# Attention with a top-1 expert layer on one core: where the softmax denominators' key sums are added, and when ScalarE takes the router's products out of PSUM

## The chip, the cores and the metric

The kernel runs on one core of a Trainium2 chip. The metric is device microseconds for one execution. Three runs of the kernel before took 587.34, 593.33 and 595.07 us; the median is 593.33 us.

## The reference

There are two stages. The first is attention with a tanh cap on the scores, over 4 batches, 12 heads, 448 positions and a head size of 64. Its output is laid out as 1792 tokens of 768 numbers. The second is a mixture of 8 experts (768 to 1024 to 768, relu) of which each token takes the best one, by the cosine between the token and an expert's embedding.

```python
def _attn_ref(q, k, v, cap) -> np.ndarray:
    scale = 1.0 / np.sqrt(q.shape[-1])
    scores = scale * np.matmul(q, k.transpose(0, 1, 3, 2))
    scores = cap * np.tanh(scores / cap)
    scores = scores - np.max(scores, axis=-1, keepdims=True)
    attn = np.exp(scores)
    attn = attn / (np.sum(attn, axis=-1, keepdims=True) + 1e-09)
    return np.matmul(attn, v).astype(np.float32)
...
    logits = xn @ en.T / tau
    expert_idx = np.argmax(logits, axis=1)
...
        h = np.maximum(x[mask] @ w1[e], 0.0)
        out[mask] = gate_w[mask, None] * (h @ w2[e])
```

All is in float32. With the cap, the maximum need not be subtracted, so the kernel takes the exponentials as they are and divides at the end.

## The kernel before, in words

**Attention.** The 48 heads are 24 pairs of heads, and two pairs make a group: 12 groups (`NH`). A group is worked off in seven blocks (`STEPS`), u = 0 to 6. Blocks 0 to 2 are the first pair's keys 0 to 383, 128 keys at a time for both heads; blocks 3 to 5 are the same for the second pair; block 6 holds the last 64 keys of both pairs. A block of `prob` is 128 keys x 2 heads x 448 queries. Keys lie on partitions, so the softmax denominator is a sum over blocks and then over partitions.

One loop over a slot number g puts the instructions of all engines in order (`manual_schedule`: what stands first in the program stands first in its engine's queue). In slot g the program issues:

- `scores(g)`: TensorE multiplies K by Q (six matmuls, from parts that VectorE splits into high and low in `split_qk`), and ScalarE takes the tanh and then the exponential. From block pair 4 on the exponential is one instruction for two blocks;
- `values(g - 4)`: TensorE adds the block's product with V in PSUM. After a group's block 6, in slot u = 3 of the next group, VectorE copies the two results out (`xt`, line 850). The two PSUM banks of results are single buffers, so the next group's first `values`, in slot u = 4, waits for that copy;
- `add_keys(g - 3)`: the key sums, below;
- up to two steps of a queue `later`: the router, its transposes, and `rows`, which transposes `xt` and scales it;
- from about group 8 on, one step of `fill`: half of a 128-row piece of the first expert's weights is split into two float16 parts, by ScalarE (line 227) and VectorE (line 228).

**Key sums.** For each pair of heads, `add_keys` makes one tile `sums` of 128 x 896. Blocks 0 and 1 are added on VectorE (line 807). Block 2 is added by a DMA that accumulates into `sums`, issued from GpSimd's queue (line 812), and so is the half of block 6 that belongs to the pair (line 821, 64 partitions). Only in the last group are blocks 5 and 6 added by VectorE and GpSimd (lines 815 and 823). A second accumulation into a tile waits for the first to land, and GpSimd's queue waits with it. A buffer of `prob` holds two blocks and there are four, so the tanh eight slots later waits until the accumulations from that buffer have landed.

**Router.** `router` (line 856) multiplies the attention output by the expert embeddings and the key sums by a column that picks them: 12 matmuls for two groups at once, or 6 for one group, eight times in all. It stands in slot u = 4 of the group after the one that it needs, behind that slot's scores and values on TensorE. ScalarE copies the product from PSUM to `ls` in the same step (line 870). `router_t`, one slot later, transposes `ls` on TensorE (lines 881, 882), and VectorE takes the reciprocal of the sums (line 886) and scales the logits. The steps after it are `rows`.

**Experts.** After attention the tokens are sorted by expert, and tiles of 128 tokens go through the two layers as float16 products in three parts. `tile0` begins the first tile at the end of attention.

Of the kernel before, what the change touches and what calls it, by code (L numbers as in the profile page):

```python
# [35 lines left out]
ALU = mybir.AluOpType  # L36
# [48 lines left out]
def attention_moe(ctx: ExitStack, tc: tile.TileContext, q, k, v, cap, emb, tau, w1, w2, qk_pairs, v_pairs, out):  # L85
    nc = tc.nc
# [189 lines left out]
    with ExitStack() as actx:  # L276
# [77 lines left out]
        NH = B * NP // 2  # L354
# [393 lines left out]
        def attention_bounded(apool, ps_s, ps_o):  # L748
# [20 lines left out]
            def block(g):  # L769
                return prob[g // 2][:, 2 * (g % 2) : 2 * (g % 2) + 2, :]  # L770
# [32 lines left out]
            def add_keys(g):  # L803
                i, u = divmod(g, STEPS)
                if u in (1, 4):
                    t = apool.tile([P, 2, S], F32, tag="sums", name=f"sums{2 * i + u // 3}", bufs=6)
                    nc.vector.tensor_tensor(t, block(g - 1), block(g), op=ALU.add)  # L807
                    sums[2 * i + u // 3] = t
                elif u in (2, 5):
                    t = sums[2 * i + u // 3]  # L810
                    if i < NH - 1 or u == 2:
                        nc.gpsimd.dma_start(out=t, in_=block(g), accum_op=ALU.add)  # L812
                    else:
                        for s, eng in enumerate((nc.vector, nc.gpsimd)):
                            eng.tensor_tensor(t[:, s, :], t[:, s, :], block(g)[:, s, :], op=ALU.add)
                elif u == STEPS - 1:
                    for n in range(2):
                        sl = slice(n * DH, (n + 1) * DH)
                        t = sums[2 * i + n]
                        if i < NH - 1:  # L820
                            nc.gpsimd.dma_start(out=t[sl], in_=block(g)[sl], accum_op=ALU.add)  # L821
                        else:
                            (nc.gpsimd if n else nc.vector).tensor_tensor(t[sl], t[sl], block(g)[sl], op=ALU.add)

            def values(g):
                i, u = divmod(g, STEPS)
# [29 lines left out]
            def router(i, n):  # L856

                d = ps_t.tile([P, 512], F32, tag="t", name=f"lp{i}")
                far = n if n == 2 else 0
                for a in range(3):  # L860
                    for m in range(n):
                        k = m + far if a else m
                        nc.tensor.matmul(  # L863
                            d[k * 32 : (k + 1) * 32, :S],
                            pick[:, a - 1, :] if a else en_t[:, (i + m) % NP, :, :].rearrange("p a e -> p (a e)"),
                            sums[i + m][:, a - 1, :] if a else xt[i + m],
                            start=a == (1 if a and far else 0), stop=a == (0 if far and not a else 2),
                        )
                ls = apool.tile([P, S], F32, tag="lrow", name=f"ls{i}", bufs=1)
                nc.scalar.copy(ls, d[:, :S])  # L870
                return ls
# [43 lines left out]
            route = []  # L915
# [16 lines left out]
            def after(i):  # L932

                tmp = {}
                (b, m), nop = divmod(i, NP // 2), lambda: None
                if m == 0:
                    return
                j, n = (2 * i - 2, 4) if m == 1 else (2 * i, 2)
                steps = [lambda: tmp.update(l=router(j, n)), lambda: router_t(j, n, tmp["l"])]
                steps += [lambda x=x: rows(x) for x in range(j, j + n)]  # L940
                if m == NP // 2 - 1:
                    steps.append(lambda: write_rows(b, 0, D))
                    if b < B - 1:
                        steps += [
                            lambda: (square_x(b, 0), square_x(b, 1), hold.extend([1] * HOLD)),
                            lambda: (square_x(b, 2), square_x(b, 3), norms_x(b), side.extend(z), hold.extend([1] * HOLD)),
                        ]
                        z = [nop, nop, lambda: (scales_x(b), route.extend(g))]
                        r = [lambda: choose(b), nop, nop, nop, lambda: rank_rows(b, rank(b))]
                        if b == B - 3:  # L950
                            r += [
                                lambda: tmp.update(m=first_expert(counts(b))),
                                lambda: (first_order(tmp["m"]), first_scales(), start_first()),
                            ]
                        if b == B - 2:
                            r.append(lambda: tmp.update(b=first_rows(counts(b))))
                        r += [lambda: (add_carry(b), token_rows(b, range(2))), lambda: token_rows(b, range(2, 4))]
                        g = [lambda: gates(b), lambda: gates_out(b)]
                        if b == B - 2:
                            g += [nop, lambda: first_table(tmp["b"])]  # L960
                        steps.insert(2, lambda: route.extend(r))
                later.extend(steps)

            with tc.manual_schedule():
# [717 lines left out]
```

## Time and profile before

| | |
|---|---|
| median of three runs | 593.33 us (587.34 to 595.07) |
| profiled execution | 591.52 us, of which the profile's span is 589.8 us |
| TensorE matmul busy in the span | 481.3 us (82%) |
| VectorE, ScalarE, GpSimd busy | 286.3, 295.6, 171.8 us |
| granted TensorE clock, mean | 0.933 of full speed |

Names in the rows: PE is TensorE's matmul, PEld its weight load, DVE VectorE, ACT ScalarE, POOL GpSimd. A number in square brackets at the end of a timeline row is the idle time of the engine just before, and what ended it. Attention runs from about 8 us to 280 us, the experts after it. In the trace, a group's block 6 is the one whose scores have line 790.

### The profile page before, as it was taken

To read this page: it belongs to the slowest core of one execution; us is meant where nothing else is said; L and a number is where in the kernel's file an instruction comes from. 1 tells how busy PE (TensorE), PEld (TensorE's weight loads), DVE (VectorE), ACT (ScalarE), POOL (GpSimd) and SP (SyncE) were. 2 spreads that over 40 slices of the span, in tenths; PEclk is the share of its full clock that TensorE was granted. 3 is DMA by queue.
4 is the path that set the end of the run, shared out by engine and by line. 5 is a ranking of instruction groups with operands and counts; after the bars stand their busy time and mean duration, and the time that the engine had idled before them with its cause. 6 is when DMAs were issued, how large, how long until landed. Compare 5 with 4: busy or idle time off the path is not lost. (4 is left out here: it accounts for less than half of the span.)

```text
span 589.8 us, 11987 instructions
## 1 busy us (share of the span) xinstructions
PE 481.3 (82%) x4621; PEld 295.7 (50%) x4622; DVE 286.3 (49%) x694; ACT 295.6 (50%) x350; POOL 171.8 (29%) x267
## 2 busy tenths in 40 slices
PE   4988893998849595575777979999999999997970
PEld 2323330343213142122646738887778887786750
DVE  4552564264634466327656591266221851295810
ACT  3975784776937498641530641173111821284500
POOL 3111212111120211414010462265322563255420
PEclk9997998899988899777979989999999999998986
DMA  7586779775993858541506992148111672096920
GB/s 206 145 182 101 158 215 228 115 162 166 171 247 88 202 189 157 125 74 55 175 5 227 396 345 108 56 163 314 55 55 56 229 287 62 31 326 236 364 100 6
DMA packets 34045, 97.06 MB, mean 165 GB/s; under 512 B 7998, under 2 KB 8282, under 8 KB 33955
## 3 DMA queue, kind: packets, MB, share of 16 engines
q1 hardware_dynamic: 24818, 66.14, 32.0%
q0 software_dynamic: 7888, 28.21, 23.7%
q10 hardware_dynamic: 1248, 1.61, 0.9%
q8 instruction: 44, 0.72, 0.5%
q14 instruction: 47, 0.38, 0.2%
HBM read 67.94 MB, written 13.00 MB: 137 GB/s over the span
## 5 line engine op out<-in xcount | busy, mean ns | idle before, releaser
L794 ACT ACTIVATE prob<-s,icap 128x896 f32<-128x896 f32 x84 | 82.5, 995 | 28.2 <-PE s L784 12.7
L237 PEld LDWEIGHTS <-h 128*128 128x128 f16 x1056 | 79.9, 99 | 11.2 <-issue 8.9
L237 PE MATMUL h<-xh,h 128*128 128x128 f16 (+1 forms) x480 | 78.7, 218 | 6.3 <-issue 4.9
L798 ACT ACTIVATE prob<-prob,cap_b 128x896 f32<-128x896 f32 (+1 forms) x57 | 79.8, 1399 | 1.9
L237 PE MATMUL h<-xl,h 128*128 128x128 f16 (+1 forms) x480 | 78.7, 218 | 1.5 <-issue 1.5
L237 PE MATMUL h<-xh,l 128*128 128x128 f16 (+1 forms) x480 | 78.7, 218 | 0.3 <-issue 0.3
L836 PE MATMUL v<-prob,vb 128*64 128x448 f32 x288 | 73.3, 589 | 4.1 <-DVE xt L850 4.1
L784 PE MATMUL s<-hi 64*128 64x448 f32 x144 | 35.4, 489 | 27.9 <-ACT prob L794 19.2
L812 POOL DMA_DIRECT2D sums<-prob x23 | 21.3, 927 | 109.0 <-DVE sums L807 25.9
L237 PEld LDWEIGHTS <-l 128*128 128x128 f16 x528 | 52.0, 99 | 0.5 <-issue 0.5
L784 PEld LDWEIGHTS s<-hi 64*128 64x128 f32 x144 | 14.2, 193 | 69.7 <-ACT prob L794 35.8
L210 POOL TENSOR_TENSOR x_tile<-xg 128x768 f32<-128x768 f32 x16 | 24.3, 1520 | 82.0 <-PE xt L218 67.7
L863 PE MATMUL lp<-sums,pick 128*32 128x448 f32 x96 | 30.0, 726 | 21.8 <-DMA sums<-prob 21.8
L1405 PE MATMUL h<-xh,h 128*128 128x160 f16 x192 | 41.0, 237 | 6.7 <-PEq L1548 4.1
L249 ACT ACTIVATE hh<-h 128x512 f16<-128x512 f32 (+1 forms) x20 | 11.5, 575 | 69.7 <-PE h L237 69.7
L221 ACT CAST xh<-xt 128x384 f16<-128x384 f32 x30 | 13.0, 482 | 64.1 <-PE xt L218 56.2
L250 DVE SCALAR_TENSOR_TENSOR hl<-h,hh 128x512 f16<-128x512 f32 (+1 forms) x20 | 13.3, 664 | 64.3 <-ACT hh L249 64.3
L643 PEld LDWEIGHTS <-hh 128*128 128x128 f16 (+1 forms) x352 | 33.3, 101 | 20.0 <-issue 2.0
L228 DVE SCALAR_TENSOR_TENSOR l<-w1r,by_pos,h 128x1024 f16<-128x1024 f32 x30 | 37.7, 1307 | 11.3 <-ACT h L227 11.3
L821 POOL DMA_DIRECT2D sums<-prob x22 | 21.0, 955 | 73.2 <-DMA sums<-prob 56.8
L1405 PE MATMUL h<-xl,h 128*128 128x160 f16 x192 | 41.1, 237 | 0.0
L1405 PE MATMUL h<-xh,l 128*128 128x160 f16 x192 | 41.1, 238 | 0.0
(309 smaller groups left out, 1037.2 us busy)
## 6 DMA issues: line engine op xcount, KB each, us to landing
w1r<-in_moe_w_dram SPq DMA_DIRECT2D x36, 512.0 KB, 6.2
w2r<-in_moe_w_dram SPq DMA_DIRECT2D x24, 768.0 KB, 7.1
sums<-prob POOLq DMA_DIRECT2D x23, 448.0 KB, 6.7
qkb<-in_qk_pairs_dram SPq DMA_DIRECT2D x11, 896.0 KB, 5.8
vb<-in_v_pairs_dram SPq DMA_DIRECT2D x12, 448.0 KB, 5.5
sums<-prob POOLq DMA_DIRECT2D x22, 224.0 KB, 4.4
x_dram<-xsb SPq DMA_DIRECT2D x4, 1152.0 KB, 5.4
ring<-in_moe_w_dram SPq DMA_DIRECT2D x6, 512.0 KB, 3.8
```

What stands on the lines that cost most here:

```text
L210: nc.gpsimd.tensor_tensor(x_tile, xg[:, :D], xg[:, SCALE : SCALE + 1].to_broadcast([P, D]), op=ALU.mult)
L228: nc.vector.scalar_tensor_tensor(out=lo, in0=raw, scalar=scale, in1=hi, op0=ALU.mult, op1=ALU.subtract, accum_out=acc)
L237: nc.tensor.matmul(hp[:, f, :W], l[j][:, c], x[:, j, :W], start=j == 0 and f == 0 and n == 0, stop=j == DC - 1 and f == 3 and n == 2, skip ...
L643: nc.tensor.matmul(y, hidden[h][l][:, c, o : o + k], w2p[p % 2][w][f // 2][:, f % 2, m * C : (m + 1) * C], start=f == 0 and n == 0, stop=f ...
L784: nc.tensor.matmul(sp[:, s, :S], l[sl, kc], r[sl, :], start=n == 0, stop=n == 2)
L794: nc.scalar.activation(o, sp[:, :, :S], AF.Tanh, scale=icap)
L798: nc.scalar.activation(o, o, AF.Exp, scale=cap_b)
L812: nc.gpsimd.dma_start(out=t, in_=block(g), accum_op=ALU.add)
L821: nc.gpsimd.dma_start(out=t[sl], in_=block(g)[sl], accum_op=ALU.add)
L836: nc.tensor.matmul(o[sl, :S], vb[:, u, sl], pt[:, s, :], start=u % 3 == 0, stop=False, skip_group_check=True)
L863: nc.tensor.matmul(d[k * 32 : (k + 1) * 32, :S], pick[:, a - 1, :] if a else en_t[:, (i + m) % NP, :, :].rearrange("p a e -> p (a e)"), su ...
L1405: nc.tensor.matmul(o, w1p[p % 2][l][j][:, c], x[:, j, :], start=j == 0 and f == fs[0] and m == 0, stop=j == DC - 1 and f == fs[-1] and m == 2,
```

## The change

All the additions of `add_keys` are put on VectorE, as `tensor_tensor` instructions, in the slots where the DMAs were issued; none is left on GpSimd or a DMA. The router's step is cut in two: the matmuls stay in their slot, and ScalarE's copy becomes a step of its own in the next one. All later steps of that queue (transposes, `rows`, the choice of experts) move by one place.

```diff
                 elif u in (2, 5):
                     t = sums[2 * i + u // 3]
-                    if i < NH - 1 or u == 2:
-                        nc.gpsimd.dma_start(out=t, in_=block(g), accum_op=ALU.add)
-                    else:
-                        for s, eng in enumerate((nc.vector, nc.gpsimd)):
-                            eng.tensor_tensor(t[:, s, :], t[:, s, :], block(g)[:, s, :], op=ALU.add)
+                    nc.vector.tensor_tensor(t, t, block(g), op=ALU.add)
                 elif u == STEPS - 1:
                     for n in range(2):
                         sl = slice(n * DH, (n + 1) * DH)
                         t = sums[2 * i + n]
-                        if i < NH - 1:
-                            nc.gpsimd.dma_start(out=t[sl], in_=block(g)[sl], accum_op=ALU.add)
-                        else:
-                            (nc.gpsimd if n else nc.vector).tensor_tensor(t[sl], t[sl], block(g)[sl], op=ALU.add)
+                        nc.vector.tensor_tensor(t[sl], t[sl], block(g)[sl], op=ALU.add)
...
+                return d
+
+            def router_c(i, d):
                 ls = apool.tile([P, S], F32, tag="lrow", name=f"ls{i}", bufs=1)
                 nc.scalar.copy(ls, d[:, :S])
                 return ls
...
-                steps = [lambda: tmp.update(l=router(j, n)), lambda: router_t(j, n, tmp["l"])]
+                steps = [
+                    lambda: tmp.update(d=router(j, n)),
+                    lambda: tmp.update(l=router_c(j, tmp["d"])),
+                    lambda: router_t(j, n, tmp["l"]),
+                ]
...
-                        steps.insert(2, lambda: route.extend(r))
+                        steps.insert(3, lambda: route.extend(r))
```

In the program of the change the lines behind `add_keys` have other numbers: 811 and 816 are the new additions, 843 is the copy `xt`, 866 the router's copy, 901 is in `rows`.

ScalarE, in the group that runs the first router, slots u = 4 to 6; `s_4`, `s_5`, `s_6` are the scores of blocks 4 to 6 of that group, `lp` the router's product. Before:

```order
L794 ACTIVATE prob_529<-s_4_530,icap 128x896
L870 COPY ls_560<-lp_547 128x448
L794 ACTIVATE prob_529<-s_5_562,icap 128x896
L798 ACTIVATE prob_529<-prob_529,cap_b 128x1792
L794 ACTIVATE prob_585<-s_6_586,icap 128x896
```

and in the change:

```order
L794 ACTIVATE prob_529<-s_4_530,icap 128x896
L794 ACTIVATE prob_529<-s_5_560,icap 128x896
L798 ACTIVATE prob_529<-prob_529,cap_b 128x1792
L866 COPY ls_572<-lp_547 128x448
L794 ACTIVATE prob_574<-s_6_575,icap 128x896
```

The copy has moved behind the next slot's tanh and the exponential of the two blocks.

VectorE, in the next group, from the first sum of slot u = 0 to the copies of slot u = 3; `xsb<-xb` is the scaling in `rows`. Before:

```order
L807 TENSOR_TENSOR sums_624<-prob_499,prob_529 128x896
L905 TENSOR_TENSOR xsb<-xb_628,inv_574 128x3x128
L905 TENSOR_TENSOR xsb<-xb_628,inv_574 64x128
L905 TENSOR_TENSOR xsb<-xb_647,inv_574 128x3x128
L905 TENSOR_TENSOR xsb<-xb_647,inv_574 64x128
L850 COPY xt_680<-v_542 128x448
L850 COPY xt_682<-v_621 128x448
```

and in the change:

```order
L807 TENSOR_TENSOR sums_617<-prob_499,prob_529 128x896
L901 TENSOR_TENSOR xsb<-xb_621,inv_583 128x3x128
L901 TENSOR_TENSOR xsb<-xb_621,inv_583 64x128
L811 TENSOR_TENSOR sums_617<-sums_617,prob_529 128x896
L901 TENSOR_TENSOR xsb<-xb_640,inv_583 128x3x128
L901 TENSOR_TENSOR xsb<-xb_640,inv_583 64x128
L816 TENSOR_TENSOR sums_545<-sums_545,prob_574 64x896
L816 TENSOR_TENSOR sums_617<-sums_617,prob_574 64x896
L901 TENSOR_TENSOR xsb<-xb_660,inv_583 128x3x128
L901 TENSOR_TENSOR xsb<-xb_660,inv_583 64x128
L843 COPY xt_680<-v_542 128x448
L843 COPY xt_682<-v_614 128x448
```

Three additions more stand ahead of the copies `xt` (the fourth of a group stands in slot u = 5), and one more step of `rows`, which came in the slots before.

## Rows read from the trace of the kernel before

**Rows 1.** The page, part 1: busy us, share of the span, instructions.

```profile
PE 481.3 (82%) x4621; PEld 295.7 (50%) x4622; DVE 286.3 (49%) x694; ACT 295.6 (50%) x350; POOL 171.8 (29%) x267
```

**Rows 2.** Windows (stretch: length, busy us by engine, clock, DMA share, GB/s).

```profile
32.55:154.23 121.68, 102.02 (x604) 38.45 (x602) 56.65 (x128) 85.74 (x85) 21.96 (x27) 0.93 0.77 170
154.23:260.91 106.68, 75.99 (x428) 26.44 (x428) 49.66 (x147) 68.93 (x79) 22.43 (x28) 0.87 0.67 155
...
310.00:589.80 279.80, 245.61 (x3148) 199.28 (x3148) 130.08 (x273) 98.21 (x127) 110.13 (x162) 0.96 0.49 180
```

**Rows 3.** Waits, whole span: who waited for whom, us in total, times, longest.

```profile
ACT ls L870 <- PE lp L863: 54.1, 8, 12.7
...
DVE inv L886 <- PE lt L882: 56.8, 7, 15.3
...
PE lp L863 <- DMA sums<-prob: 21.8, 11, 6.3
...
PE s L784 <- ACT prob L794: 19.2, 13, 6.7
...
ACT prob L794 <- DMA sums<-prob: 12.5, 3, 8.0
```

**Rows 4.** Timeline of the longest router: start, us, instruction, [idle before, releaser].

```profile
172.29 0.59 DVE L763 CAST hi<-qkb 128x832 fp32r<-128x832 f32 x1 [6.43 <-DMA qkb<-in_qk_pairs_dram]
...
177.35 3.11 PE L863 MATMUL lp<-sums,pick 128*32 128x448 f32 x10 [1.10 <-DMA sums<-prob]
...
180.39 0.47 PE L784 MATMUL s<-hi 64*128 64x448 f32 x2
```

**Rows 5.** Windows of seven routers, first product to next scores; columns as above.

```profile
112.64:116.32 3.68, 3.29 (x27) 0.80 (x25) 2.07 (x3) 2.01 (x2) 0.98 (x2) 1.00 0.32 31
...
244.89:258.48 13.59, 7.93 (x26) 1.30 (x24) 0.78 (x1) 0.95 (x1) 2.97 (x5) 0.63 0.79 138
sum 55.38, PE 33.62 PEld 6.44 DVE 12.93 ACT 10.92 POOL 10.24; mean PE 4.80 PEld 0.92 DVE 1.85 ACT 1.56 POOL 1.46
```

**Rows 6.** Timeline of the shortest router.

```profile
114.72 1.66 PE L863 MATMUL lp<-sums,pick 128*32 128x448 f32 x10 [0.39 <-DMA sums<-prob]
```

**Rows 7.** Timeline: scores behind a tanh that waited for an accumulation.

```profile
45.53 0.74 PE L784 MATMUL s<-hi 64*128 64x448 f32 x2 [3.74 <-ACT prob L794]
...
103.53 0.74 PE L784 MATMUL s<-hi 64*128 64x448 f32 x2 [6.67 <-ACT prob L794]
```

**Rows 8.** Groups of instructions, VectorE: xcount, busy us, mean ns, idle before.

```profile
L764 DVE TENSOR_TENSOR lo<-qkb,hi 128x832 fp32r<-128x832 f32 x24 | 24.6, 1026 | 0.8
...
L228 DVE SCALAR_TENSOR_TENSOR l<-ring,first_s,h 128x384 f16<-128x384 f32 (+1 forms) x28 | 21.8, 786 | 20.6 <-ACT h L227 20.6
...
L905 DVE TENSOR_TENSOR xsb<-xb,inv 128x384 f32<-128x384 f32 (+1 forms) x48 | 17.4, 412 | 6.1 <-PE xb L901 6.1
...
L763 DVE CAST hi<-qkb 128x832 fp32r<-128x832 f32 x24 | 14.0, 582 | 8.5 <-DMA qkb<-in_qk_pairs_dram 8.5
...
L807 DVE TENSOR_TENSOR sums<-prob 128x896 f32<-128x896 f32 x12 | 13.0, 1084 | 0.0
...
L870 ACT COPY ls<-lp 128x448 f32<-128x448 f32 x8 | 4.3, 534 | 54.1 <-PE lp L863 54.1
...
L823 DVE TENSOR_TENSOR sums<-sums,prob 64x896 f32<-64x896 f32 x1 | 1.1, 1076 | 0.0
```

**Rows 9.** Window of one group with VectorE densely filled.

```profile
209.30:226.28 16.98, 13.83 (x96) 5.68 (x95) 14.94 (x49) 16.72 (x24) 1.71 (x2) 1.00 0.75 227
```

**Rows 10.** Timeline of the last group's additions.

```profile
268.39 2.09 POOL L823 TENSOR_TENSOR sums<-sums,prob 64x896 f32<-64x896 f32 x1 [0.72 <-DVE sums L815]
...
268.75 2.14 DVE L228 SCALAR_TENSOR_TENSOR l<-ring,first_s,h 128x384 f16<-128x384 f32 x1
...
275.77 0.96 PE L863 MATMUL lp<-xt,en_t 128*32 128x448 f32 x2 [6.29 <-DVE xl L222]
```

**Rows 11.** DMA issues: KB each, median us to landing.

```profile
sums<-prob POOLq DMA_DIRECT2D x23, 448.0 KB, 6.7
```

## The prediction

> **What bounds the kernel now.** I read the busy times first, to see which engine could be the bound. TensorE is busy for 82% of the span, VectorE for 49%, ScalarE for 50%, GpSimd for 29% [rows 1]. A mean over stages says little, so next come the windows [rows 2]. From 310 us on, in the experts, TensorE is busy for 245.6 of 279.8 us, and no line of the change runs there; I take that stage as shifted, not changed. The attention groups lie in two windows: 32.55 to 154.23 us, without the splitting of the first expert's weights (`fill`), and 154.23 to 260.91 us, with it. In the first TensorE is busy for 102.0 of 121.7 us, in the second only for 76.0 of 106.7 us, and there the granted clock has fallen to 0.87. No engine fills the second window: it is a stage of waits.
>
> The table of waits names them [rows 3]. TensorE stood for 21.8 us in the router's matmuls, waiting for a DMA that accumulates the key sums, and for 19.2 us in scores, waiting for ScalarE's tanh to free a PSUM buffer; ScalarE's tanh itself waited 12.5 us for such a DMA, because the block of `prob` was still being read. The two longest rows, ScalarE's copy waiting for the router (54.1 us) and VectorE waiting for the transposes (56.8 us), are consequences: both engines stand because TensorE is held in the router. The timeline of the longest router shows the chain and its second price: the last matmuls ran only at 177.35, took 3.11 us for ten that need 1.66 us in another router, and the next scores began at 180.39 [rows 4, 6]. The half-speed stretch, after a wait, has a granted clock of 0.63 over another such router [rows 5].
>
> **The change part by part, against the profiled execution of 591.52 us.**
>
> *Routers.* From a router's first matmul to the next scores, seven of the eight took 55.38 us together [rows 5]. The shortest, with 12 matmuls, took 3.68 us of which 0.39 us was a wait [rows 5, 6], so 3.29 us is the price without one; I take it for all seven, though some have 6 matmuls. The last sums that a router needs are issued two slots before it. As a VectorE addition they take 1.08 us each [rows 8] in place of a DMA that lands after 6.7 us [rows 11], behind another one for which GpSimd's queue waits. So the wait goes: 55.38 - 7 x 3.29 = 32.3 us gained. The lower end is nothing, if other lateness holds the routers; the upper end is this sum, as nothing below 3.29 us was seen.
>
> *Tanh held by an accumulation.* TensorE lost 3.74 us and 6.67 us behind it [rows 7]. With an addition that ends in its own slot or the next, and a buffer that is wanted five slots after, this goes: 10.4 us, the upper end 12.5 us [rows 3], the lower nothing.
>
> *The additions on VectorE.* 23 whole additions of 1.084 us and 22 of half the partitions, which cost as much (1.076 us), and in the last group about 1 us more, are 49.6 us of new VectorE work [rows 8]. What hides it is VectorE's idle time. In the first window it was busy for 56.7 us, and gets six groups of 4.32 us: 82.6 us in a window that shrinks to some 106 us, 78%. In the second, 49.7 + 17.3 = 67 us in some 79 us, 85% [rows 2]. The densest group shows 14.94 of 16.98 us, 88%, at full clock [rows 9], so it fits, but narrowly. What is late next is the copy `xt` in slot u = 3, for which the next values wait. Between the transposes and that copy VectorE now does four steps of `rows` (two instructions of 412 ns each, 3.3 us), a split of 1.61 us, four additions of 4.3 us and, with `fill`, three splits of 786 ns: 11.6 us, or 9.2 us without `fill` [rows 8]. Its cover is four slots, 9.7 us at the pace of 16.98 us for seven [rows 9]. So about 2 us late in each of the four groups with `fill` and 0.5 us in the six others: a loss of 11 us. The ends are nothing, and all 49.6 us.
>
> *The copy one slot later.* Eight copies of 534 ns [rows 8] only change place. In slot u = 5 ScalarE cannot begin the tanh before TensorE has left the router, so the copy's wait of 54.1 us held back nothing, and its going gains nothing. The later copy ends a slot before the transposes want it; if ScalarE were a slot behind, each would cost its 0.53 us, 3.7 us for seven. I take nothing.
>
> *What the freed DMA queues do.* VectorE waited 6.43 us for a load of Q and K while the router was held [rows 4]; with that router short, this load is the next to be late. It arrived at 172.3, and a router that ends at 170 needs its split about two slots later, some 174: hidden by about nothing. With fewer transfers beside it, it may come earlier. I take nothing, with 3 us lost as the other end.
>
> *Last group.* There GpSimd's additions go, which ran beside a VectorE split of 2.14 us that takes 0.79 us elsewhere, and the last router waited 6.29 us for VectorE [rows 8, 10]. VectorE gets 1 us more and loses the slow split. I take 2 us gained, between nothing and 6.3 us. The Trainium skill ("SBUF — State Buffer", section on the two sides of SBUF) says that a VectorE instruction with two SBUF inputs and a GpSimd instruction that reads SBUF exclude one another. The slow split beside GpSimd's addition agrees, but by that rule the new additions of this group stand behind GpSimd's scaling of the next tile, and the term would be near nothing; the sum would be 2 us worse.
>
> *Sum:* 32.3 + 10.4 - 11 + 2 = 33.7 us gained, 591.52 - 33.7 = 557.8 us. The median of the three runs is 1.8 us above this execution, so 559.6; I predict **560 us**, 5.6% less than 593.33.
>
> **The rivals.**
>
> *VectorE runs out (0.20).* It takes its instructions in order and stands for long in every transpose wait [rows 3], so 85% may not be reached. If it is kept busy for only 70% of the two windows, they need (82.6 + 67) / 0.70 = 213.7 us instead of 228.4, a gain of 14.7: about 577 us, 578 on the median. For it speaks that its mean now is 47%; against it the densest group with 88%, in which it still kept up. The Trainium skill ("Perfetto Trace Analysis", section on optimizing Scalar and DVE operations) advises to take work off VectorE where it is saturated; this change does the reverse. By that rule the time is this rival's, or the next one's.
>
> *Slower, by the same engine (0.05).* The point that decides is 149.6 / 228.4 = 65.5%: below it, VectorE's order costs more than the DMAs did. At 60% the windows take 249.3 us, 21 us more: about 614 us. What would do it are copies `xt` and the splits of Q and K late in every group. For it: in the densest group VectorE stood still for only 16.98 - 14.94 = 2.0 us [rows 9], half of the 4.3 us that each group gets. Against it: the other groups have more, 121.7 - 56.7 = 65 us in six of them [rows 2].
>
> *The change does not free the routers (0.09).* The sums could be late for another reason: the exponential of the block, or VectorE being held in the transposes, with the additions behind them. Then the tanh's 10.4 us go but most of the routers' 32.3 us stay, and the delays of 11 us come on top: 591.5 + 1.8 - 10.4 + 11 - 2 = 592, no change. Against it: the additions stand two slots before the router, and no transposes lie between.
>
> **How the numbers follow.** The forecast, with 0.66, is 545 to 573: the sum, with the late copies between nothing and twice my price and the last group between nothing and 6.3 us. The range 545 to 582 takes in the first rival and leaves out the last two rivals above (0.14) and some 0.05 below, where more goes than I counted. About 2%, 12 us, is what a measurement of this kernel can tell from no change. Faster by more, under 581.5 us: the forecast and most of the first rival, 0.83. Within 2%: the third rival and a rest of the first, 0.12. Slower: 0.05.
>
> **What will show it.** Right: no wait of the router for the sums, seven routers of 3 to 4 us, no tanh behind an accumulation, the second window (block 6 of the eighth group to that of the last) of 80 to 90 us with a clock above 0.9, VectorE busy for some 336 us in all, and a copy of the router with next to no wait. The price is right if TensorE's values wait for `xt` by about 10 us in total. Wrong: the same windows with VectorE over 90% busy, waits of scores for `hi` or `lo`, or routers that still wait.

## The result, and the profile after

The change took **537.69 us** (median of four runs, 533.27 to 540.43) beside 591.59 us for the kernel before on the same chip: a ratio of 0.9085, with a 95% interval of 0.8989 to 0.9181. In a later set of runs it was 538.1 us beside 592.1 us, 0.908 (0.9031 to 0.9129); that median is of five runs, and a sixth, of 543.5 us, is left out as in the slower state. The direction was right; the time lies below the low end of the range, 545. The profiled execution took 539.73 us with a span of 538.0 us, 51.8 us less than before.

The busy times after, in the columns of [rows 1]:

```profile
PE 465.1 (86%) x4621; PEld 293.9 (55%) x4622; DVE 332.8 (62%) x740; ACT 294.5 (55%) x350; POOL 132.1 (25%) x220
```

VectorE has 46.5 us more, near the 49.6 us priced. But TensorE has 16.2 us **less**, for the same 4621 matmuls. Of these, 15.1 us lie in the seven routers (33.62 us busy before, 18.52 after, below); for the rest the prediction had no term.

The same three stretches after, by the same marks (block 6 of the second, eighth and last group); the columns are those of [rows 2]:

```profile
32.54:130.06 97.52, 90.66 (x600) 35.74 (x598) 80.17 (x148) 84.24 (x81) 1.16 (x2) 1.00 0.37 128
130.06:215.14 85.08, 69.13 (x431) 25.44 (x429) 67.80 (x166) 67.86 (x80) 7.97 (x9) 0.88 0.35 117
215.14:538.00 322.86, 281.61 (x3465) 222.16 (x3463) 162.60 (x381) 119.00 (x167) 118.21 (x174) 0.96 0.47 169
```

and, for the third, the row of before:

```profile
260.91:589.80 328.89, 280.33 (x3460) 220.81 (x3459) 161.81 (x378) 117.60 (x164) 119.89 (x174) 0.95 0.46 165
```

Against [rows 2] the first window lost 24.2 us, the second 21.6, the last 6.0. In the first the clock rose from 0.93 to 1.00 of full speed, and TensorE's busy time fell from 102.0 to 90.7 us for the same products. Of these 11.4 us, 6.3 are in the window's four routers, three of which had the full clock before too; the other 5.1 us go with the higher clock, that is, with fewer stretches at the lower of the two levels.

The waits that answer to [rows 3]:

```profile
ACT ls L866 <- PE lp L856: 4.7, 1, 4.7
...
DVE inv L882 <- PE lt L878: 20.7, 6, 6.2
...
PE v L829 <- DVE xt L843: 17.1, 7, 5.4
...
PE s L784 <- ACT prob L794: 3.3, 6, 1.3
```

No router waits for sums and no tanh for a DMA. The scores' waits for the tanh went from 19.2 us [rows 3], and 5.2 us more at line 790, to 3.3 us. The price is in the third row: TensorE's values wait 17.1 us for `xt`, 4.1 us before.

The routers after, from the first product to the next scores, as in [rows 5]; the first four lie in the first window, and the sum is of all seven:

```profile
43.38:45.78 2.40, 2.40 (x27) 0.68 (x26) 2.27 (x3) 1.86 (x2) 0.00 (x0) 1.00 0.03 7
61.40:63.04 1.64, 1.64 (x14) 0.39 (x12) 1.61 (x3) 1.61 (x2) 0.00 (x0) 1.00 0.04 10
93.34:95.73 2.39, 2.39 (x26) 0.68 (x24) 2.32 (x4) 2.13 (x2) 0.00 (x0) 1.00 0.12 2
110.70:112.34 1.64, 1.64 (x15) 0.39 (x14) 1.60 (x3) 1.08 (x2) 0.00 (x0) 1.00 0.00 0
146.68:151.18 4.50, 4.50 (x27) 1.00 (x25) 3.12 (x3) 1.59 (x2) 0.00 (x0) 0.52 0.07 4
...
sum 18.52, PE 18.52 PEld 4.54 DVE 16.80 ACT 10.16 POOL 2.17; mean PE 2.65 PEld 0.65 DVE 2.40 ACT 1.45 POOL 0.31
```

Before, the three others of the first window, beside the 3.68 us of [rows 5]:

```profile
48.64:53.18 4.54, 4.23 (x28) 0.99 (x26) 0.00 (x0) 0.45 (x1) 0.85 (x2) 0.79 1.01 147
68.03:72.89 4.86, 3.36 (x14) 0.67 (x12) 2.08 (x3) 2.20 (x2) 0.90 (x1) 1.00 0.65 83
131.16:136.35 5.19, 3.45 (x14) 0.67 (x12) 2.08 (x3) 1.23 (x2) 1.02 (x2) 1.00 0.72 94
```

In every router after, TensorE's busy time is the whole length. At full clock twelve matmuls take 2.40 us and six take 1.64; the fifth takes 4.50 at a granted clock of 0.52, near the lower of the two levels (1.2 of 2.4 GHz); 1.7 us ahead of it TensorE had waited 3.26 us for `xt`. The timeline of the first shows why the router of [rows 6] was not a price without a wait:

```profile
43.38 0.96 PE L856 MATMUL lp<-xt,en_t 128*32 128x448 f32 x8
...
44.16 1.69 PE L856 MATMUL lp<-sums,pick 128*32 128x448 f32 x16
...
45.78 0.47 PE L784 MATMUL s<-hi 64*128 64x448 f32 x2
```

The sixteen rows on the sums are one run of 1.69 us here. In [rows 6] the last ten of them alone took 1.66 us, and in another router before, at full clock too, the last six:

```profile
71.30 1.66 PE L863 MATMUL lp<-sums,pick 128*32 128x448 f32 x6 [1.50 <-DMA sums<-prob]
```

The records of the single matmuls show why. The router's products go to four quarters of a PSUM tile (`d[k * 32 : (k + 1) * 32]`), and TensorE works on the four side by side: in the change four records start within 0.02 us, the next four 0.38 to 0.40 us later, and six such turns are the 2.40 us. When one tile of sums is late, the last four records of its quarter run alone, for 1.6 us. In [rows 6] the fourth quarter was 1.29 us behind the other three (114.72 beside 113.43), which is the 3.68 us less 2.40; only 0.39 us of it is idle time, because the other quarters were still at work. So a router's busy time can hold a wait.

**Where the 51.8 us came from.** In each window I split off the routers' stretches, and outside them TensorE's busy time from the rest, in which it stands (first window before: 121.68 - 18.27 of routers - 87.69 busy = 15.72; after: 97.52 - 8.07 - 82.59 = 6.86).

| part | before | after | change | predicted |
|---|---|---|---|---|
| seven routers | 55.38 | 18.52 | -36.9 | -32.3 |
| first window, standing outside routers | 15.72 | 6.86 | -8.9 | -10.4 + 3 (`xt`, my price for this window) |
| second window, standing outside routers | 12.87 | 15.95 | +3.1 | +8 (`xt`) |
| both windows, busy outside routers | 144.39 | 141.27 | -3.1 | 0 |
| after the last group's block 6 | 328.89 | 322.86 | -6.0 | -2 |
| sum | | | -51.8 | -33.7 |

Each column is one profiled execution. In another one of the change the two windows took 180.1 us in place of 182.6, and the last stretch 326.9 in place of 322.9.

### The profile page after: what moved, and what is told of

Read it like the earlier page. It is cut to its first block, busy times and chain, and to the rows that moved or that the text cites. A ratio compares the mean times of both kernels' runs of the same rounds, so it can differ in the third digit from the quotient of the medians.

```text
span 538.0 us, 11859 instructions
## 1 busy us (share of the span) xinstructions
PE 465.1 (86%) x4621; PEld 293.9 (55%) x4622; DVE 332.8 (62%) x740; ACT 294.5 (55%) x350; POOL 132.1 (25%) x220
## 5 line engine op out<-in xcount | busy, mean ns | idle before, releaser
L829 PE MATMUL v<-prob,vb 128*64 128x448 f32 x288 | 73.3, 588 | 17.2 <-DVE xt L843 17.1
L392 POOL TENSOR_TENSOR den<-den,half_b 128x4 f32<-128x4 f32 x4 | 4.1, 1030 | 200.8 <-ACT junk L389 200.8
L250 DVE SCALAR_TENSOR_TENSOR hl<-h,hh 128x512 f16<-128x512 f32 (+1 forms) x20 | 13.3, 663 | 64.4 <-ACT hh L249 64.4
L222 DVE TENSOR_TENSOR xl<-xt,xh 128x384 f16<-128x384 f32 x30 | 15.3, 550 | 44.5 <-ACT xh L221 44.5
L643 PE MATMUL y<-h,hl 128*128 128x384 f16 (+1 forms) x160 | 38.2, 329 | 2.0 <-DVE hl L250 2.0
```

The source lines that it names most:

```text
L222: nc.vector.tensor_tensor(lo, t, hi, op=ALU.subtract)
L250: nc.vector.scalar_tensor_tensor(out=c, in0=a, scalar=0.0, in1=b, op0=ALU.max, op1=ALU.subtract, accum_out=acc[:, h : h + 1])
L643: nc.tensor.matmul(y, hidden[h][l][:, c, o : o + k], w2p[p % 2][w][f // 2][:, f % 2, m * C : (m + 1) * C], start=f == 0 and n == 0, stop=f ...
L829: nc.tensor.matmul(o[sl, :S], vb[:, u, sl], pt[:, s, :], start=u % 3 == 0, stop=False, skip_group_check=True)
```

## The experiments

The theory was that of the prediction: the sums by DMA came late, and this held the routers and the tanh; VectorE's order gives part of it back in waits for `xt`; the router's copy in its later slot does nothing. The rivals gave the gain to the copy, to one block's additions alone, or to GpSimd and the DMA queues being free. Each median stands beside runs of the kernel before on the same chip (591.3 to 592.1 us).

### One half of the change alone

**The additions alone**, with ScalarE's copy in its old slot:

```diff
-                steps = [
-                    lambda: tmp.update(d=router(j, n)),
-                    lambda: tmp.update(l=router_c(j, tmp["d"])),
-                    lambda: router_t(j, n, tmp["l"]),
-                ]
+                steps = [lambda: tmp.update(l=router(j, n)), lambda: router_t(j, n, tmp["l"])]
```

> All key sums on VectorE as in the change, but the router's copy stays in the router's slot, as before. Theory 1 (the whole gain comes from the accumulating DMAs; moving the copy is neutral): 536 to 543 us, like the change. Theory 2 (moving the copy and with it ScalarE's squares by a slot relieves ScalarE; the 24 us in which scores waited for the tanh fell to 3 us by that): 545 to 555 us, with scores waiting for the tanh for 10 us or more.

Measured: 534.13 us (531.49 to 536.7), ratio 0.8996 (0.894 to 0.9053). Its waits:

```profile
ACT ls L863 <- PE lp L856: 18.7, 7, 8.6
...
PE v L829 <- DVE xt L843: 12.0, 6, 3.6
...
PE s L784 <- ACT prob L794: 4.5, 5, 2.0
```

The whole gain is in the additions; the time is 1.9 us under the first theory's range. ScalarE again stands before its copy, for 18.7 us, and the time shows no cost of it. TensorE's wait for `xt` is 12.0 us, 5 us less than in the change.

**The copy alone**, one slot later, with the DMAs of before (the other half of the diff):

> The key sums by DMA as before, only the router's copy one slot later. Theory 1: 585 to 596 us, no change, and the router still waits 20 us or so for the accumulations. Theory 2: 575 to 583 us, with the wait of scores for the tanh down by 8 us or more.

Measured: 589.58 us (585.5 to 593.28), ratio 0.9964 (0.9924 to 1.0003). The router's wait for the sums stands where it was:

```profile
PE lp L863 <- DMA sums<-prob: 24.0, 10, 6.4
...
PE s L784 <- ACT prob L794: 16.1, 7, 4.5
```

With the sums late, the copy's slot is worth nothing that can be told from no change.

### One block's additions alone

**Only block 6** by VectorE; blocks 2 and 5 stay DMAs that accumulate, and the copy keeps its old slot:

```diff
-                        if i < NH - 1:
-                            nc.gpsimd.dma_start(out=t[sl], in_=block(g)[sl], accum_op=ALU.add)
-                        else:
-                            (nc.gpsimd if n else nc.vector).tensor_tensor(t[sl], t[sl], block(g)[sl], op=ALU.add)
+                        nc.vector.tensor_tensor(t[sl], t[sl], block(g)[sl], op=ALU.add)
```

> Only the additions of block 6 are moved to VectorE; blocks 2 and 5 stay accumulating DMAs, and the router's copy stays in its slot. Theory 1, with the second accumulation of a tile (which waits for the first to land and holds GpSimd's queue) as the main cause: 545 to 560 us, the router's wait under 5 us. Rival (the first accumulation is itself late, and now VectorE waits for it in its own queue): 565 to 590 us, with VectorE waiting for the accumulations for 15 us or more.

Measured: 591.65 us (587.85 to 595.18), ratio 0.9989 (0.9959 to 1.002), just above the rival's range. The routers no longer wait, but VectorE does, in order, before block 6:

```profile
DVE sums L820 <- DMA sums<-prob: 61.3, 12, 9.3
...
PE v L833 <- DVE xt L847: 60.9, 11, 11.7
```

The accumulation of block 2 or 5 had not landed when VectorE wanted to add block 6; the copy `xt` stood behind that addition, and TensorE behind the copy, for 60.9 us in place of 21.8 us in the router [rows 3]. So the first accumulation is late too, not only the second: block 5's is issued one slot ahead of that addition, some 2.4 us by [rows 9], and in this run the accumulations landed 4.6 us after their issue (median of 23). A wait moved to a busy in-order queue costs more than in the router.

**Only blocks 2 and 5** by VectorE, block 6 by DMA:

```diff
-                    if i < NH - 1 or u == 2:
-                        nc.gpsimd.dma_start(out=t, in_=block(g), accum_op=ALU.add)
-                    else:
-                        for s, eng in enumerate((nc.vector, nc.gpsimd)):
-                            eng.tensor_tensor(t[:, s, :], t[:, s, :], block(g)[:, s, :], op=ALU.add)
+                    nc.vector.tensor_tensor(t, t, block(g), op=ALU.add)
```

> Only the additions of blocks 2 and 5 are moved to VectorE; the halves of block 6 stay accumulating DMAs, and the router's copy stays in its slot. Theory 1 with the chain of two accumulations as the cause: one accumulation alone is issued two slots before the router and lands 4.4 us later, so a wait of about 1 us in each of seven routers: 542 to 552 us. Rival (each accumulation near the router is late by itself): 560 to 575 us, the router still waiting 10 us or more.

Measured: 549.9 us (548.83 to 553.69), ratio 0.9299 (0.9235 to 0.9362).

```profile
PE lp L859 <- DMA sums<-prob: 9.8, 5, 5.3
```

This half alone brings most of the gain, about 41 us, and leaves the routers a wait of 9.8 us. The halves do not add up: 41 and nothing make 57 together. Block 6 alone brings nothing because its addition stands, on VectorE, behind the accumulation of block 5; with that one on VectorE too, it brings the other 16.

### When the additions are issued

**All additions one slot earlier**, with the copy in its old slot:

```diff
-                    if 0 <= g - 3 < last_step:
-                        add_keys(g - 3)
+                    if 0 <= g - 2 < last_step:
+                        add_keys(g - 2)
```

> All sums on VectorE, the router's copy in its old slot (as in the first experiment, 534 us), and every addition one slot earlier than there, so that fewer stand in front of the copies xt. Theory (what is left of VectorE's price is the lateness of xt, 12.0 us of values waiting for it): 526 to 531 us, that wait under 6 us. Rival (the earlier addition meets an exponential that isn't done and holds VectorE's queue): 534 to 545 us, VectorE waiting for ScalarE's exponential for 10 us or more.

Measured: 531.31 us (526.73 to 534.16), ratio 0.8997 (0.8943 to 0.9051); against the kernel of the additions alone that is no difference by the ratios. Two of its waits, and the second window:

```profile
PE s L784 <- ACT prob L794: 7.9, 6, 3.0
...
PE v L829 <- DVE xt L843: 6.8, 4, 2.2
```

```profile
129.68:206.06 76.38, 64.42 (x427) 25.27 (x428) 66.05 (x165) 68.72 (x79) 9.87 (x11) 0.96 0.39 130
```

The wait for `xt` falls from 12.0 to 6.8 us (under 6 expected), and the scores' wait rises from 4.5 to 7.9. VectorE is 86% busy in that window.

**Block 6's additions behind the copy `xt`:**

```diff
-                    if 0 <= g - 3 < last_step:
+                    if 0 <= g - 3 < last_step and (g - 3) % STEPS != STEPS - 1:
                         add_keys(g - 3)
...
+                    if j >= 0 and j % STEPS == STEPS - 1:
+                        add_keys(j)
```

> As the first experiment, but the two additions of block 6 stand behind the copies xt, one slot later. Theory (xt is late because of what stands in front of it): the wait of values for xt under 5 us instead of 12.0, the router waits for its sums 1 us or less in each of seven cases: 525 to 531 us. Rival (the router now waits for as much): 533 to 540 us, with the router waiting for VectorE for 7 us or more.

Measured: 537.86 us (536.5 to 538.87), ratio 0.9097 (0.9052 to 0.9142). That is in the rival's range and 3.7 us above the additions alone, with intervals that just meet; the profiled executions took 536.5 and 536.7 us. So it is no faster. TensorE's wait for `xt` was 3.6 us in all, and the edit did what it was for; but the first window grew from 97.91 to 102.42 us. The additions alone, and then this kernel:

```profile
32.56:130.47 97.91, 92.12 (x605) 36.37 (x603) 81.69 (x149) 85.10 (x85) 1.96 (x3) 0.98 0.37 128
```

```profile
32.04:134.46 102.42, 96.82 (x604) 37.17 (x602) 83.39 (x150) 85.42 (x85) 1.96 (x3) 0.98 0.35 122
```

TensorE stands no longer there (102.42 - 96.82 = 5.6 us, against 97.91 - 92.12 = 5.8 us for the additions alone), but its busy time is 4.7 us more, at the same mean clock of 0.98. The four routers of this window hold it: they take 3.15, 3.34, 3.34 and 3.35 us, at full clock, beside 2.39, 1.64, 2.39 and 1.64. They wait for the sums, as the rival said. The weight loads show this, and so do the last products of the second router:

```profile
PEld lp L856 <- DVE sums L816: 7.3, 10, 1.0
```

```profile
62.61 1.69 PE L856 MATMUL lp<-sums,pick 128*32 128x448 f32 x6 [0.18 <-DVE sums L816]
```

Again most of the wait lies inside TensorE's busy time. What the later place gained at `xt`, the routers lost.

### How much VectorE has left

**The new work doubled:** behind each of the 48 instructions one more of its size, which takes the maximum of `sums` with itself and changes nothing.

```diff
                     nc.vector.tensor_tensor(t, t, block(g), op=ALU.add)
+                    nc.vector.tensor_tensor(t, t, t, op=ALU.max)
...
                         nc.vector.tensor_tensor(t[sl], t[sl], block(g)[sl], op=ALU.add)
+                        nc.vector.tensor_tensor(t[sl], t[sl], t[sl], op=ALU.max)
```

> As the first experiment, with each of the 48 moved additions followed by an instruction of the same size on VectorE (the maximum of the sum with itself, which changes nothing): 52 us more of VectorE. Theory (VectorE was near its limit after the change: 80 of 97 and 68 of 85 us busy in the two windows, so this can't be hidden): 565 to 580 us, attention bound by VectorE at 88% or more. Rival (VectorE's idle time is ample and only the lateness of xt costs): 540 to 552 us.

Measured: 584.81 us (582.83 to 588.67), ratio 0.989 (0.9824 to 0.9957), above both ranges. VectorE's busy time rose by 52.1 us to 386.6, and the time by 50.7 us:

```profile
36.68:159.25 122.57, 100.96 (x605) 37.84 (x603) 108.10 (x173) 86.39 (x84) 2.27 (x4) 0.89 0.29 102
```

```profile
PE v L831 <- DVE xt L845: 44.8, 11, 6.1
```

The first such portion raised the wait for `xt` by 8 us over before; the second costs nearly its whole length. It adds 32.8 us to that wait (44.8 beside 12.0) and 14.4 us to TensorE's busy time (480.6 beside 466.2), at a lower mean clock (0.89 in this window, 0.98 there). VectorE then is busy for 108.10 of 122.57 us, 88%, and in the second window for 84.76 of 98.60 us, 86%. The share alone does not tell when it costs: [rows 9] showed 88% in a group at full clock, and the additions one slot earlier have 86% in the second window above. The Trainium skill ("Perfetto Trace Analysis", section on optimizing Scalar and DVE operations) advises to take work off VectorE where it is saturated. This run agrees for the second portion; the change itself, with VectorE at 80.17 of 97.52 us (82%) in this window, was not there yet.

### What the DMAs cost besides

**The additions alone, with 45 small DMAs** of 16 bytes a partition from GpSimd's queue, one where each accumulation stood:

```diff
+                    if i < NH - 1 or u == 2:
+                        send()
...
+                nc.gpsimd.dma_start(out=spare[:, n, :], in_=half_b)
```

> As the first experiment, with 45 small DMAs (16 bytes for each of 128 partitions) issued from GpSimd's queue where the accumulations stood; nothing reads what they write. Theory (the end of the program, behind the last output, takes 0.1 us longer for each DMA that GpSimd has issued: its last drain took 6.77 us with 45 accumulations, 4.97 with 23, 4.89 with 22, 3.09 with none): the drain at 6.8 us again and 537 to 541 us, attention unchanged. Rival (the drain depends on what the accumulations moved, not on their number): drain at 3.1 us, 532 to 536 us.

Measured: 544.32 us (541.76 to 545.96), ratio 0.9193 (0.9139 to 0.9247), 10 us more than without and above both ranges. Attention is unchanged (the last group's block 6 at 212.01 us, 212.11 without). The last instruction of each program, first in this kernel (span 542.9), then in the additions alone (span 535.0):

```profile
529.59 1.09 POOL L684 DMA_INDIRECT out_dram<-yo,idx_out  x1 [2.23 <-DVE redo_i L1517]
```

```profile
526.05 1.10 POOL L684 DMA_INDIRECT out_dram<-yo,idx_out  x1 [2.92 <-DVE redo_i L1506]
```

From there to the end it takes 13.3 us with the DMAs and 8.95 without. Before and in the change it is the same pair, first before (span 589.8), then after (span 538.0):

```profile
576.01 1.08 POOL L684 DMA_INDIRECT out_dram<-yo,idx_out  x1 [1.53 <-DVE redo_i L1513]
```

```profile
529.44 1.10 POOL L684 DMA_INDIRECT out_dram<-yo,idx_out  x1 [2.41 <-DVE redo_i L1513]
```

13.8 and 8.6 us. The records of GpSimd's sequencer in the traces show where this lies, in its last drain and the semaphore step ahead of it:

| kernel | accumulating or small DMAs | last drain, us | step before, us |
|---|---|---|---|
| before; copy alone | 45 | 6.77 | 1.81 |
| 45 small DMAs | 45 | 6.77 | 1.82 |
| block 6 alone; blocks 2 and 5 alone | 23; 22 | 4.97; 4.89 | 1.37; 1.36 |
| change; additions alone | 0 | 3.09 | 0.92 |

So each of these DMAs that GpSimd issues adds about 0.1 us to the end of the program, accumulations and small ones alike: 4.6 us for 45. The rest of the 10 us lies in the experts and between executions, and was not taken apart. No run put back the accumulations' traffic without their waits (a DMA share of 0.77 in the first window [rows 2], 0.37 after), so what the freed queues bring besides is not tested; TensorE's one wait for a split of Q and K is 8.2 us before and 7.8 in the change, both times at the start.

### The slot again, with the additions early, and the last group

The last runs share one chip. **The change with all additions one slot earlier** (the edit above, made in the change itself):

> The change as it is, with every addition of the key sums issued one slot earlier. Theory 1 (the late slot of the router's copy changes nothing; what is left of the VectorE price is the copies xt standing behind additions, and an earlier slot takes part of it away): TensorE waits for xt some 7 to 10 us instead of 17, the second window takes 76 to 80 us instead of 85, median 527 to 536 us, within 4 us of the kernel with the additions earlier and the copy in its old slot. Rival (the later slot has a price of its own, because all steps of the queue behind it stand one slot closer to the copies xt): the wait for xt stays at 12 us or more and the time is 535 to 540 us, 5 us or more above that kernel.

**The additions alone, one slot earlier**, again:

> The additions alone, one slot earlier, the router's copy in its old slot, timed again beside the change itself. Theory 1: 526 to 535 us, 3 to 9 us (0.6 to 1.7%) under the change. Rival (its lead over the change was chance between two chips): within 2 us of the change.

**The change again:**

> The change itself again, on the chip of the other kernels of this call, as their comparison: 533 to 541 us by every theory.

Measured: 537.86 us (536.03 to 541.41), ratio 0.9079 (0.9039 to 0.9118), for the first; **531.17 us** (527.76 to 533.42), 0.8958 (0.8914 to 0.9001), for the second; 538.1 us, 0.908 (0.9031 to 0.9129), for the change. The intervals of the second and the other two do not meet: with the additions on VectorE one slot earlier, the later slot of the copy costs 6.7 us, 1.3%. So my theory that it does nothing is refuted for this kernel, though it holds where the sums are late. Its time is the rival's, its wait for `xt` not quite; the waits of the first and then of the second:

```profile
PE v L829 <- DVE xt L843: 10.1, 6, 4.4
```

```profile
PE v L829 <- DVE xt L843: 6.9, 4, 2.2
```

3.2 us more, as between the change and the additions alone (17.1 and 12.0). The later slot also moves each step of `rows` one slot closer to the copies. In the first kernel one more wait stands out on the timeline:

```profile
93.05 0.23 ACT L433 ACTIVATE ex<-lg 128x32 f32<-128x32 f32 x1 [4.45 <-DVE lg L432]
...
94.22 0.49 PE L784 MATMUL s<-hi 64*128 64x448 f32 x2 [3.79 <-ACT prob L794]
```

ScalarE stands in the gates for a small VectorE result that is behind additions, and TensorE loses 3.79 us. These two would make about the size of the difference, but the windows put it elsewhere. The profiled executions took 539.6 and 531.7 us. The first window is 3.5 us longer (100.85 and 97.31 us), the second 1.0 us shorter (79.99 and 81.01), and 5.7 us lie after the last group's block 6, here for the first kernel and then for the second:

```profile
213.13:539.60 326.47, 284.46 (x3465) 224.09 (x3463) 162.71 (x381) 119.10 (x167) 118.08 (x171) 0.95 0.47 167
```

```profile
210.92:531.70 320.78, 280.39 (x3460) 221.35 (x3459) 160.40 (x379) 117.57 (x164) 115.13 (x171) 0.95 0.48 169
```

Of the 5.7 us, 2.1 are on the way from that block to the first expert tile (18.1 and 16.0 us), where the transposes and the steps of `rows` also come one slot later. The other 3.6 us are in the experts, which differ by as much between two executions of the change. So the cost of the later slot is measured, and where it lies is shown only in part.

**The last group's additions divided between VectorE and GpSimd again**, on the kernel of the additions alone, as in the rows of the diff with `nc.gpsimd` and `NH - 1`:

> The additions alone with the copy in its old slot (534.1 us before), except that the last group's last additions are divided between VectorE and GpSimd again, as in the kernel before. Theory of the prediction (2 us of the last group came from VectorE's split no longer running beside GpSimd's additions): one split of line 228 takes some 2.1 us again, and the way from the last group's block 6 to the first expert tile is 1.5 to 3 us longer; 535 to 538 us. Rival (the slow split lies beside a wait that is there anyway, so the term was nothing): the split is slow again but the way is within 1 us of what it was; 532 to 536 us. By both, GpSimd's end of the program stays short, since no DMA of it comes back.

Measured: 537.79 us (533.13 to 540.76), ratio 0.9088 (0.9037 to 0.9139). The split is slow again, and the first expert tile begins at

```profile
218.18 2.14 DVE L228 SCALAR_TENSOR_TENSOR l<-ring,first_s,h 128x384 f16<-128x384 f32 x1
...
228.34 0.29 PE L237 MATMUL hp<-xh,h 128*128 128x128 f16 x1
```

18.0 us after the last group's block 6 (210.34), and 17.5 us after it (212.11) in the additions alone:

```profile
229.64 0.29 PE L237 MATMUL hp<-xh,h 128*128 128x128 f16 x1
```

So the slow split is worth 0.5 us, as its rival said; but the median is the theory's, 3.7 us higher than in the other set of runs, with intervals that overlap a little, and nothing in the rows explains it.

## Why the prediction was right in kind and wrong in size

1. **Routers: right, 4.6 us too small.** Taking the additions off the DMAs ended the router's wait. The price of 3.29 us without a wait was too high: 2.40 us for twelve matmuls and 1.64 for six at full clock. "Nothing below 3.29 us was seen" was true and no bound: that router held more waiting than the 0.39 us that its row named (1.29 us, in one quarter), and three of the seven have half the matmuls, which I noted and then did not use. The forecast for routers was 3 to 4 us; five of the seven took less.
2. **Tanh held by an accumulation: the step that failed most.** I counted the two waits behind an accumulation, 10.4 us, with 12.5 as the upper end. All the waits of scores for the tanh were 24.4 us, and 21.1 of them went, 10.7 more than the term. The other waits did not name a DMA as their releaser, so they looked like another cause; but they went when the DMAs went, and stayed when only the copy moved (16.1 us at line 784). I take them for after-effects of engines set back together, which is inferred from which kernels have them; the chain from one to the other was not followed. It is also not the DMAs alone: with 23 accumulations left (block 6 by VectorE) they were 2.1 us, as TensorE stood before `xt` instead.
3. **VectorE's additions: right in kind, the size partly luck.** The waits for `xt` rose by 13.0 us, 11 forecast; they are 17.1 us in all, where about 10 was to show that the price was right. And the 11 us hold a slip: 9.2 us of work under a cover of 9.7 us are 0.5 us early, not late, so the working gives 8 us, all of it in the four groups with `fill`. Measured, 13.4 of the 17.1 us lie in those four groups of the second window, though the first of them has no split yet (the first split begins at 157.97 us), and 3.7 us in the others, where the slip had put 3. The window's utilisation was forecast at 78% and 85%, and is 82% and 80%. One row shows such a group, just ahead of the copy:

```profile
187.25 2.20 DVE L816 TENSOR_TENSOR sums<-sums,prob 64x896 f32<-64x896 f32 x2
...
190.83 1.76 PE L829 MATMUL v<-prob,vb 128*64 128x448 f32 x4 [5.40 <-DVE xt L843]
```

4. **The copy one slot later: taken as nothing, costs.** With the sums late it is nothing; beside the additions one slot earlier it takes 6.7 us. With the additions in their own slot the change lies 3.6 us above the additions alone, in different sets of runs whose intervals overlap. I had its bound (3.7 us) from ScalarE being late; what it met, as far as is shown, was VectorE's order and the last group.
5. **Clock: missing.** I priced waits, and left the matmuls at the length they had. TensorE's busy time fell from 33.62 us [rows 5] to 18.52 in the routers, and by 3.1 us outside them in the two windows; only the second is missing from the sum. The first is not all clock. There were stretches at the lower level (3.11 us for ten in [rows 4], 1.66 in [rows 6]), but three routers at a clock of 1.00 were busy for 3.29, 3.36 and 3.45 us before, and the routers of the change at that clock for 2.40 or 1.64. Outside the routers, in the first window TensorE stands less (6.86 us for 15.72), the clock went from 0.93 to 1.00 and the busy time fell by 5.1 us; in the second it stands more (15.95 us for 12.87), the clock stayed at 0.88, where I had forecast above 0.9, and the busy time rose by 2.0 us.
6. **After the last group: 6.0 us in place of 2, for another reason.** The way from the last group's block 6 to the first expert tile did not get shorter: 18.0 before, 18.8 after. What is shown of the gain is GpSimd's end of the program, 4.6 us by the table of drains, on which I had no row; in the other execution of the change the whole term is 2.0 us in place of 6.0. The slow split, from which I had the 2 us, was worth 0.5. In the change an addition that takes 1.08 us elsewhere takes 2.24 beside GpSimd's scaling:

```profile
211.26 1.55 POOL L210 TENSOR_TENSOR x_tile<-xg 128x768 f32<-128x768 f32 x1 [2.92 <-DMA xg<-x_dram,idx_in]
...
211.52 2.24 DVE L811 TENSOR_TENSOR sums<-sums,prob 128x896 f32<-128x896 f32 x1
```

The Trainium skill ("SBUF — State Buffer", section on the two sides of SBUF) has VectorE instructions with two SBUF inputs and GpSimd's that read SBUF exclude one another; this row agrees, and so does the term near nothing that the prediction worked out by that rule. The slow instruction only changed its place.

The rivals: VectorE did not run out, though one more portion of the same size shows that it was near; it got slower in no run of the change; and the routers were freed. All my errors but two small ones (`xt`, the copy) went one way, since the terms took only the waits whose cause I could name and left the follow-on waits, the clock and the end of the program at nothing.

The best version is neither kernel of the pair: the additions on VectorE one slot earlier, with the router's copy in its old slot, takes 531.2 us, 10.4% under before and 1.3% under the change in the same set of runs. From the additions alone at their own slot (534.1 us in another set of runs) the ratios do not tell it apart.

## What to carry to other kernels

When a stall on an in-order machine goes, count all waits of the stalled engine in that stage and ask which would remain, not only those that name the culprit; and take the price of the work from its instructions at full clock, not from its best instance in a stage full of waits. Where an engine works on several pieces side by side, its busy time can hold a wait too. The first 46 us of work moved to an engine that is about half busy brought 13 us of waits, the next 52 us cost their full length, and the share of busy time did not show the limit, so test the headroom by doubling the new work. Half of a fix can bring nothing, when the other half still feeds an in-order queue.

## What the runs showed of the hardware

- GpSimd's end of the program grows by 0.1 us for each of these DMAs that it has issued, the accumulations and small ones of 16 bytes a partition alike: 8.6 us for the last drain and the step ahead of it with 45 of them, 6.3 with 22 or 23, 4.0 without.
- Four of the router's matmuls with weights of 128x32, into four quarters of a PSUM tile, run side by side: four records start within 0.02 us and the next four 0.38 to 0.40 us later, at full clock. With one quarter late, its last four records took 1.6 us alone, and of its 1.29 us of lateness 0.39 us show as idle time.
- The DMAs that accumulate were late even without another into the same tile before them: VectorE stood 61.3 us, twelve times, for the first accumulation into a tile, with 4.6 us from issue to landing (median of 23).
- The experts' stage, which no line of the change touches, differed between two executions of the change by 4 us (322.86 and 326.88 us after the last group's block 6), so a term of a few us there needs medians, not two profiles.
